# The second product of the plain chunks reads w_out in straight rows, and the columns are ordered on the way out, with a new table for the order of work

## Chip, core and metric

The kernel runs on one core of one Trainium2 chip. The metric is the time of one execution in microseconds, as the device sees it; the number for a kernel is the median of its runs. Beside the timed runs there is one execution under the profiler, whose trace the rows below are from.

## What is computed

Linear attention without softmax, an RMS norm per head, and a two-layer network with the gate h * cos(h). All inputs are float32: q, k, v of 8 x 8 x 576 x 64, w_in of 512 x 2048, w_out of 2048 x 512.

```python
kv = np.einsum('bhsd,bhse->bhde', k, v)
out = np.einsum('bhsd,bhde->bhse', q, kv)
rms = np.sqrt(np.mean(out * out, axis=-1, keepdims=True) + 1e-06)
attn = out / rms * g_norm
x = attn.transpose(0, 2, 1, 3).reshape(4608, 512)
h = x @ w_in
g = h * np.cos(h)
result = g @ w_out
```

## The kernel before

**Tiles.** The 4608 rows of x are nine chunks of 512 (`CH`), the inner width of 2048 is 16 blocks of 128 (`NJ`, index j), and a result is written in tiles of 128 rows x 512 columns (index t, four to a chunk). The float32 values are split into a high and a low part of type float32r (`hi`, `lo`), and each product is three matmuls: high by high, high by low, low by high. One such triple streams 512 columns three times.

**Stages.** Chunks 0 to 2 (`PLAIN = 3`) are done step by step: `stage1_part` makes h for one block j (the bank of its own, `bank` in the trace), `act_part` makes g = h * cos(h) and splits it into `ghi` and `glo`, and `stage2_part` adds g times the block of w_out into four PSUM banks `acc0` to `acc3`. Chunks 0 and 1 are cut into two segments each, since w_in and w_out are still being loaded: the first segment's result is stored in DRAM (`part`), and at the end of the second it is loaded again and added (`out_part` with `before`). Chunks 3 to 8 form three pairs. Their first product (`quad_part`) is done for two chunks at once by a scheme of seven products for eight blocks; its triples carry `bank<-wi,wo` in the trace, since its weight products are kept in the buffers named `wo` and its combinations of x in those named `wi`. The second product of chunks 3 to 6 (`gather_part`) is plain again, as in `stage2_part`; that of the last pair, chunks 7 and 8, goes through `turned_unit`, where w_out is the stationary operand and g the moving one.

**w_out's columns.** `w_part` converts each block of w_out from its 64-bit words and splits it; for w_out it writes `hi` and `lo` with the 16 groups of 32 columns in another order (a and b exchanged, 4 x 4), which the turned pair wants. The plain second product undoes this as it reads: `by_column(w[:, s, :])` is an access of 4 x 4 runs of 32 elements, and `acc` holds the columns in order. `out_part` then scales `acc` into a tile `slot` on ScalarE (or on DVE, added to `slot`, where there is a first part) and stores it; `t_slot` has five such tiles, which the norms of x and the sums of weights use as well. A tile goes back only when its store has landed.

**Order.** The order of instructions on each engine and of the DMA issues on SP is worked out by a planner in the kernel itself (`Order`), with a cost in us for each step (0.68 for a triple of matmuls of either product), a due time `due(i)`, and an offset for each step from the table `haste` (`put_off`). `grid` rounds the planned times, `sched.busy` holds the time from which an engine is free. What the planner decides is fixed: every instruction is issued in program order on its engine, through the one line 239 (`Pinned`), so in the trace all have the line L239, and groups are told apart by their tiles' names. `warm_part(16)` issues 64 matmuls on zeros into `acc2` at the front, where nothing else is ready. `sums_part` forms the sums of blocks of w_in for the quads.

Of the kernel before, what the change touches and what calls it, by code (L numbers as in the profile page):

```python
# [20 lines left out]
P = 128  # L21
# [29 lines left out]
def grid(t):  # L51
    return math.floor(t * 1e4 + 0.5) / 1e4
# [133 lines left out]
def tile_kernel(  # L186
# [42 lines left out]
    sched.busy["SP"] = sched.busy["DMA"] = 1.0  # L229
# [17 lines left out]
    def act_us(f=CH):  # L247
        return 0.1 + f / 1200
# [71 lines left out]
    def due(i):  # L320
# [7 lines left out]
        ('acc', 10): -397.3, ('acc', 11): 485.7, ('acc', 13): 49.6, ('acc', 14): 28.2, ('acc', 15): 71.1,  # L328
        ('acc', 16): -266.2, ('acc', 17): -172.1, ('acc', 18): 13.0, ('acc', 19): 2084.8, ('acc', 20): 23.3,
        ('acc', 21): 63.5, ('acc', 22): -52.9, ('acc', 23): 83.0, ('acc', 24): 343.6, ('acc', 25): 87.6,  # L330
        ('acc', 26): 343.7, ('acc', 27): 140.1, ('acc', 28): -2.0, ('acc', 29): 311.3, ('acc', 3): 389.0,
        ('acc', 30): -2.1, ('acc', 31): -258.8, ('acc', 32): -73.3, ('acc', 33): 146.9, ('acc', 34): -416.8,
        ('acc', 35): -518.1, ('acc', 36): -7.7, ('acc', 37): 434.6, ('acc', 38): 7.4, ('acc', 39): -253.4,
        ('acc', 4): -4.9, ('acc', 40): -84.3, ('acc', 41): 114.5, ('acc', 42): -117.7, ('acc', 43): 872.7,
        ('acc', 45): 464.5, ('acc', 46): 150.6, ('acc', 47): 168.2, ('acc', 5): -103.0, ('acc', 6): 292.7,
        ('acc', 7): -6.3, ('acc', 8): 205.3, ('acc', 9): 2.6, ('act', 0): 18.4, ('act', 1): -25.5,
        ('act', 10): 161.8, ('act', 11): 31.6, ('act', 12): -151.2, ('act', 13): -18.6, ('act', 14): -417.1,
        ('act', 15): -20.1, ('act', 16): -112.5, ('act', 17): -2.7, ('act', 18): -69.9, ('act', 19): 114.6,
        ('act', 2): -130.9, ('act', 20): -37.8, ('act', 21): 189.3, ('act', 22): -1.6, ('act', 23): 29.1,
        ('act', 24): -36.1, ('act', 25): -18.7, ('act', 26): 63.5, ('act', 27): -272.7, ('act', 28): -1.2,  # L340
        ('act', 29): 348.9, ('act', 3): -36.3, ('act', 30): -20.4, ('act', 31): 32.0, ('act', 32): -75.3,
        ('act', 33): 823.6, ('act', 34): -1.3, ('act', 35): -46.6, ('act', 36): -315.4, ('act', 37): 20.3,
        ('act', 38): -1.9, ('act', 39): 52.2, ('act', 4): 36.6, ('act', 41): 72.1, ('act', 42): 77.9,
        ('act', 43): 21.2, ('act', 44): -13.8, ('act', 45): -87.8, ('act', 46): 7.3, ('act', 47): -0.7,
        ('act', 5): -2.9, ('act', 6): -4.1, ('act', 7): 8.1, ('act', 8): -37.5, ('act', 9): 477.3,
        ('cross', 0, 0): 444.4, ('cross', 0, 1): 11.9, ('cross', 1, 0): 298.7, ('cross', 1, 1): 5.8,
        ('cross', 2, 0): -741.2, ('cross', 2, 1): -35.7, ('gate keep in', 0): -27.4, ('gate keep in', 1): 31.8,
        ('gate keep in', 10): -70.6, ('gate keep in', 11): 17.5, ('gate keep in', 12): -309.9,
        ('gate keep in', 13): -166.9, ('gate keep in', 14): 32.5, ('gate keep in', 15): -943.7,
        ('gate keep in', 2): -15.3, ('gate keep in', 4): 52.1, ('gate keep in', 5): 75.3,  # L350
        ('gate keep in', 6): 51.3, ('gate keep in', 7): -157.6, ('gate keep in', 8): -0.9,
        ('gate keep in', 9): -72.9, ('gate keep out', 0): 95.2, ('gate keep out', 1): 16.6,
        ('gate keep out', 10): 81.3, ('gate keep out', 11): 64.0, ('gate keep out', 12): 97.4,
        ('gate keep out', 13): -312.6, ('gate keep out', 14): -22.6, ('gate keep out', 15): -462.5,
        ('gate keep out', 2): -16.3, ('gate keep out', 3): -49.3, ('gate keep out', 4): 40.5,
        ('gate keep out', 5): -119.3, ('gate keep out', 6): 152.4, ('gate keep out', 7): 179.5,
        ('gate keep out', 8): 129.8, ('gate keep out', 9): 41.7, ('gate kv', 2): -38.9, ('gate kv', 3): 10.8,
        ('gate kv', 4): 20.0, ('gate kv', 5): -17.5, ('gate kv', 6): 56.5, ('gate kv', 7): -31.4,
        ('gate load', 2): -250.8, ('gate load', 3): -274.1, ('gate load', 4): -3.9, ('gate load', 5): 103.0,
        ('gate load', 6): -113.5, ('gate load', 7): -73.9, ('gate sums', 0): 22.8, ('gate sums', 2): 69.6,  # L360
        ('gate sums', 3): 3.0, ('gate sums', 4): -258.7, ('gate sums', 5): -3.5, ('gate sums', 6): 13.8,
# [1682 lines left out]
```

## Time and profile before

| | us |
|---|---|
| median of 3 timed runs | 878.9 (878.8 to 879.05) |
| the profiled execution | 875.54 |
| its span, first to last instruction | 873.8 |
| TensorE busy | 833.7 |
| DVE, ScalarE, POOL busy | 684.0, 521.0, 315.8 |

Times in rows are in us from the start of the span unless marked ns. A busy TensorE is counted as a union of pipelined matmuls, so the mean duration of one matmul is longer than the distance from one to the next; the distance is read from stretches of the chain. An engine executes in order, and an idle time is put down to what ended it.

### The profile page before, as it was taken

How to read it: one execution, taken by the hardware profiler on the slowest of the kernel's cores; microseconds unless marked ns; L12 is line 12 of the kernel's file. 1: busy time of each engine (PE TensorE's matmuls, PEld its weight loads, DVE VectorE, ACT ScalarE, POOL GpSimd, SP SyncE). 2: the span in 40 equal slices, each digit the busy share in tenths (PEclk: the TensorE clock that was granted, in tenths of full speed). 3: DMA queues.
4: the chain of work that ended last, by engine and by line, in shares of the span. 5: the costliest groups of instructions: out<-in, count | busy, mean ns of one | idle time of the engine just before them, and what ended most of it. 6: DMA issues, size and time to landing. Idle time of an engine off the chain costs nothing.

```text
span 873.8 us, 13064 instructions
## 1 busy us (share of the span) xinstructions
PE 833.7 (95%) x4392; PEld 676.0 (77%) x4392; DVE 684.0 (78%) x1034; ACT 521.0 (60%) x1019; POOL 315.8 (36%) x221
## 2 busy tenths in 40 slices
PE   7899999998998998999998999999998899999996
PEld 6678887887886886778886788878885788888875
DVE  2899997358576687766899898999679777788885
ACT  4789874346444565655677675786556555566550
POOL 2410044615436655000154482222157446553220
PEclk9999999999999999999999999999999999999999
DMA  9996255376773456779978856876566779796587
GB/s 307 304 399 243 83 163 177 122 199 175 225 192 111 124 169 218 216 253 357 271 217 223 257 171 181 230 230 194 179 195 206 237 205 298 262 342 195 171 286 192
DMA packets 175089, 191.70 MB, mean 219 GB/s; under 512 B 83376, under 2 KB 137136, under 8 KB 175024
## 3 DMA queue, kind: packets, MB, share of 16 engines
q1 hardware_dynamic: 173600, 190.04, 70.1%
q10 hardware_dynamic: 1424, 0.85, 0.3%
q8 instruction: 34, 0.56, 0.3%
q14 instruction: 31, 0.25, 0.1%
HBM read 143.66 MB, written 47.19 MB: 218 GB/s over the span
## 4 chain that ended last, share of the span: by engine, by line
PE 72%; DVE 12%; DMA 7%; ACT 4%; issue 3%; POOL 1%; SPq 0%; DVEq 0%; ACTq 0%; POOLq 0%
PE acc L239 37%; PE bank L239 35%; DVE sg L239 2%; DVE r L239 2%; DMA wo<-wod 2%; DMA wod<-wo 2%; DMA wo<-wq 2%; DVE wo L239 2%; DVE wi L239 1%; DVE glo L239 1%; DMA out_dram<-slot 1%; DVE m L239 1%; DVE qT L239 1%; DVE xhi L239 1%; DVE xlo L239 1%
## 5 line engine op out<-in xcount | busy, mean ns | idle before, releaser
L239 PE MATMUL acc<-wo,ghi 128*128 128x512 f32 x896 | 283.9, 398 | 4.2 <-DMA wo<-wod 3.0
L239 PE MATMUL bank<-wi,wo 128*128 128x512 f32 (+2 forms) x1092 | 245.6, 380 | 10.4 <-DMA wo<-wq 3.8
L239 PEld LDWEIGHTS bank<-wi,wo 128*128 128x128 f32 (+2 forms) x1092 | 190.1, 184 | 57.2 <-ACT wi L239 3.7
L239 PEld LDWEIGHTS acc<-wo,ghi 128*128 128x128 f32 x896 | 167.6, 189 | 44.1 <-issue 3.4
L239 POOL TENSOR_TENSOR rinv<-ms,mhalf 128x16 f32<-128x16 f32 (+1 forms) x36 | 97.9, 2721 | 280.1 <-DVE ms L239 278.4
L239 PE MATMUL acc<-wo,glo 128*128 128x512 f32 x448 | 178.3, 398 | 2.0 <-DVE glo L239 2.0
L239 PE MATMUL bank<-xhi,wi 128*128 128x512 f32 x320 | 102.4, 401 | 6.5 <-DVE r L239 3.9
L239 PEld LDWEIGHTS acc<-wo,glo 128*128 128x128 f32 x448 | 84.5, 189 | 23.1 <-DVE glo L239 2.8
L239 PEld LDWEIGHTS bank<-xhi,wi 128*128 128x128 f32 x320 | 60.8, 192 | 21.2 <-DVE r L239 4.3
L239 ACT ACTIVATE ki<-wi 128x512 int32<-128x512 f32 x72 | 45.1, 627 | 39.9 <-DVE wi L239 32.6
L239 DVE TENSOR_TENSOR wi<-bank,wi 128x512 f32<-128x512 f32 x72 | 49.0, 683 | 22.9 <-PE bank L239 16.6
L239 PE MATMUL bank<-xlo,wi 128*128 128x512 f32 x160 | 63.9, 400 | 0.0
L239 ACT ACTIVATE ki<-bank 128x512 int32<-128x512 f32 x72 | 42.6, 591 | 29.2 <-PE bank L239 20.4
L239 ACT COPY wi<-bank 128x512 f32<-128x512 f32 x72 | 42.0, 583 | 22.6 <-PE bank L239 19.7
L239 DVE SCALAR_TENSOR_TENSOR r<-bank,ki 128x512 f32<-128x512 f32 x49 | 33.5, 684 | 26.9 <-ACT ki L239 26.5
L239 DVE TENSOR_TENSOR glo<-r,ghi 128x512 fp32r<-128x512 f32 x55 | 44.5, 811 | 10.6 <-ACT ghi L239 10.3
L239 DVE TENSOR_TENSOR glo<-wo,ghi 128x512 fp32r<-128x512 f32 x46 | 38.3, 833 | 15.3 <-ACT ghi L239 15.1
L239 ACT CAST ghi<-wo 128x512 fp32r<-128x512 f32 x53 | 32.7, 618 | 27.8 <-PE acc L239 27.3
L239 ACT ACTIVATE r<-r 128x512 f32<-128x512 f32 x59 | 37.2, 630 | 16.8 <-DVE r L239 16.6
L239 ACT CAST ghi<-r 128x512 fp32r<-128x512 f32 x56 | 34.5, 618 | 20.2 <-PE acc L239 16.0
L239 ACT ACTIVATE wo<-wo 128x512 f32<-128x512 f32 x54 | 33.6, 630 | 21.1 <-DVE wo L239 21.0
L239 DVE TENSOR_TENSOR r<-r,bank 128x512 f32<-128x512 f32 x49 | 33.2, 678 | 8.4 <-ACT r L239 7.9
(217 smaller groups left out, 1447.5 us busy)
## 6 DMA issues: line engine op xcount, KB each, us to landing
wo<-wq SPq DMA_DIRECT2D x84, 512.0 KB, 4.3
wo<-wod SPq DMA_DIRECT2D x64, 512.0 KB, 4.5
wo<-in_moe_w_out_dram SPq DMA_DIRECT2D x16, 512.0 KB, 9.1
wi<-in_moe_w_in_dram SPq DMA_DIRECT2D x16, 512.0 KB, 9.2
wod<-wo SPq DMA_DIRECT2D x16, 512.0 KB, 3.9
wo<-wsum SPq DMA_DIRECT2D x32, 256.0 KB, 4.1
out_dram<-slot SPq DMA_DIRECT2D x28, 256.0 KB, 3.1
wq<-wi SPq DMA_DIRECT2D x24, 256.0 KB, 3.3
```

What stands on the lines that cost most here:

```text
L239: return lambda *a, **kw: tc.keep_in_program_order(f(*a, **kw))
```

## The change

`w_part` stays as it is, so w_out still lies in the exchanged order. The plain second product (in `stage2_part` and in `gather_part`) now reads it straight, `w[:, s, :]`, and `acc` holds exchanged columns. `out_part` puts them in order: on ScalarE one instruction reads `acc` in 4 x 4 runs of 32 and writes `slot` straight; on DVE, where a first part is added, four instructions take 128 columns each. A branch of `out_part` for chunk 8 is taken out. In `sums_part` a test is written in another way. `warm_part` gets 12 for 16. In the planner the rounding, the start values of SP and DMA and three costs of loads change, and the whole table `haste` is another (two lines of each stand here).

```diff
--- before.py
+++ after.py
@@ -49,7 +49,7 @@
 
 
 def grid(t):
-    return math.floor(t * 1e4 + 0.5) / 1e4
+    return math.floor(t * 1e4 + 0.43) / 1e4
 
 
 class Order:
@@ -226,7 +226,7 @@
     ps_s = ctx.enter_context(tc.tile_pool(name="ps_s", bufs=1, space=bass.MemoryType.PSUM))
 
     sched = Order()
-    sched.busy["SP"] = sched.busy["DMA"] = 1.0
+    sched.busy["SP"], sched.busy["DMA"] = 0.75, 1.9
 
     class Pinned:
 
@@ -325,156 +325,155 @@
 
 
     haste = {
-        ('acc', 10): -397.3, ('acc', 11): 485.7, ('acc', 13): 49.6, ('acc', 14): 28.2, ('acc', 15): 71.1,
-        ('acc', 16): -266.2, ('acc', 17): -172.1, ('acc', 18): 13.0, ('acc', 19): 2084.8, ('acc', 20): 23.3,
...
+        ('acc', 0): 14.0, ('acc', 1): -140.7, ('acc', 10): -107.5, ('acc', 11): -138.5, ('acc', 12): -36.8,
+        ('acc', 13): 292.5, ('acc', 14): -16.0, ('acc', 15): -12.0, ('acc', 16): 97.5, ('acc', 17): -604.7,
...
     }
 
     def put_off(*key):
@@ -603,7 +602,7 @@
                 if b:
                     yield copies(t[0:SP], heads.rearrange("h (p i) d -> p h i d", i=SQ), 1.1)
                 else:
-                    yield copies(t, heads.rearrange("h (p i) d -> (h p) i d", i=SF), 0.78)
+                    yield copies(t, heads.rearrange("h (p i) d -> (h p) i d", i=SF), 0.95)
         return pieces
 
     def first_loads():
@@ -626,7 +625,7 @@
                 copies(
                     qb[32 * e:32 * e + 32, o0 // 32:(o0 + n) // 32, :],
                     q[b, 2 * p + e // 2, s0:s0 + n, 32 * (e % 2):32 * (e % 2) + 32].rearrange(
-                        "(tb t) d -> t tb d", t=32), 0.14 + 0.18 * n / CH)
+                        "(tb t) d -> t tb d", t=32), 0.14 + 0.178 * n / CH)
                 for b, s0, o0, n in chunk_parts(c) for e in range(4)]
         return pieces
 
@@ -647,7 +646,7 @@
             for i, x in enumerate(pairs):
                 q_tiles[c, x] = qn[:, 2 * i:2 * i + 2]
             if c == 0:
-                yield copies(qn, q[0, heads, 0:CH, :].rearrange("h (r a) d -> r h a d", a=NTT), 0.78)
+                yield copies(qn, q[0, heads, 0:CH, :].rearrange("h (r a) d -> r h a d", a=NTT), 0.82)
             for b, r0, r1, m in front_rows(c):
                 if c:
                     r0 = (S - CH) // 2 if b and not m else r0
@@ -1202,10 +1201,6 @@
 
     accs = {}
 
-    def by_column(w):
-
-        return w.rearrange("p (b a r) -> p a b r", a=4, b=4)
-
     def stage2_part():
         for i, (c, j, first, final) in enumerate(steps):
             yield "wait", [w_done["wo", j], g_done[i]]
@@ -1220,7 +1215,7 @@
                 cols = slice(t * P, (t + 1) * P)
                 for n, (gt, s) in enumerate(((ghi, 0), (ghi, 1), (glo, 0))):
                     pe.matmul(
-                        out=accs[t], lhsT=gt[:, cols], rhs=by_column(w[:, s, :]),
+                        out=accs[t], lhsT=gt[:, cols], rhs=w[:, s, :],
                         start=(first and n == 0), stop=(final and n == 2),
                     )
                 if final:
@@ -1239,35 +1234,27 @@
 
     partial = {}
 
+    def by_column(acc):
+
+        return acc.rearrange("p (b a r) -> p a b r", a=4, b=4)
+
+    def in_order(o):
+        return o.rearrange("p (a b r) -> p a b r", a=4, b=4)
+
     def out_part(c, t, acc, complete, prio):
         before = partial.pop((c, t), None)
-        ends = c == NCH - 1
-        if ends and t == NTT - 1:
-
-            cut = DM // 2
-            halves = []
-            for _ in range(2):
-                slot = yield "take", t_slot, prio
-                halves.append(slot_tile(slot)[:, 0:cut])
-            yield "run", [("ACT", act_us(cut))], prio
-            act.activation(out=halves[0], in_=acc[:, 0:cut], func=AF.Copy, scale=OUT_SCALE)
-            act.dma_start(out=rows(c, t)[:, 0:cut], in_=halves[0])
-            yield "run", [("DVE", dve_us(cut))], prio
-            dve.tensor_scalar(out=halves[1], in0=acc[:, cut:], scalar1=OUT_SCALE, scalar2=None, op0=ALU.mult)
-            sp.dma_start(out=rows(c, t)[:, cut:], in_=halves[1])
-            return
         slot = yield "take", t_slot, prio
         o = slot_tile(slot)
         if before is not None:
             yield from dmas([copies(o, before, 0.85)], prio)
-            _, end = yield "run", [("DVE", dve_us(DM))], prio
-            dve.scalar_tensor_tensor(out=o, in0=acc, scalar=OUT_SCALE, in1=o, op0=ALU.mult, op1=ALU.add)
-        elif ends and t == NTT - 2:
-            _, end = yield "run", [("DVE", dve_us(DM))], prio
-            dve.tensor_scalar(out=o, in0=acc, scalar1=OUT_SCALE, scalar2=None, op0=ALU.mult)
+            for b in range(4):
+                _, end = yield "run", [("DVE", dve_us(P))], prio
+                whole = in_order(o)[:, :, b]
+                dve.scalar_tensor_tensor(
+                    out=whole, in0=by_column(acc)[:, :, b], scalar=OUT_SCALE, in1=whole, op0=ALU.mult, op1=ALU.add)
         else:
             _, end = yield "run", [("ACT", act_us(DM))], prio
-            act.activation(out=o, in_=acc, func=AF.Copy, scale=OUT_SCALE)
+            act.activation(out=in_order(o), in_=by_column(acc), func=AF.Copy, scale=OUT_SCALE)
         sched.give(t_acc[t], end)
         to = rows(c, t)
         if not complete:
@@ -1418,10 +1405,10 @@
             yield "run", [("POOL*", pool_us(WH))], prio
             pool.tensor_tensor(out=out, in0=a, in1=b, op=ALU.subtract)
         kept = []
-        for t, places in ((rest, (S2, S3)), (even, (S1, A22))):
-            slot = spare if t is rest else (yield "take", t_slot, prio)
+        for t, own, places in ((rest, spare, (S2, S3)), (even, None, (S1, A22))):
+            slot = own if own is not None else (yield "take", t_slot, prio)
             yield "run", [("ACT", act_us())], prio
-            if t is rest:
+            if own is not None:
                 hi = two(pair, [P, CH], F32R, 1)
             else:
                 hi = at.tile([P, CH], F32R, name=f"slot{slot}", bufs=1)
@@ -1896,7 +1883,7 @@
                 cols = slice(t * P, (t + 1) * P)
                 for n, (gt, s) in enumerate(((ghi, 0), (ghi, 1), (glo, 0))):
                     pe.matmul(
-                        out=accs[t], lhsT=gt[:, cols], rhs=by_column(w[:, s, :]),
+                        out=accs[t], lhsT=gt[:, cols], rhs=w[:, s, :],
                         start=(j == 0 and n == 0), stop=(j == NJ - 1 and n == 2),
                     )
                 if j == NJ - 1:
@@ -1943,7 +1930,7 @@
             t = due(begin[c]) - 24 + 1 * p if c else -10.0 + 0.5 * p
             sched.spawn(kv_front_part(c, p, t + put_off("kv", c, p)))
             sched.spawn(x_front_part(c, p, t + put_off("x", c, p)))
-    sched.spawn(warm_part(16))
+    sched.spawn(warm_part(12))
     for key in sorted(need, key=lambda x: (need[x], x)):
         t = due(need[key]) - 14.0 + put_off("load", *key)
         load(t, [w_in[key]], w_loads(key), wait=lent.get(key, ()))
```

## Rows read from the trace of the kernel before

**Rows 1.** The page's busy times, with shares of the span and instructions.

```profile
PE 833.7 (95%) x4392; PEld 676.0 (77%) x4392; DVE 684.0 (78%) x1034; ACT 521.0 (60%) x1019; POOL 315.8 (36%) x221
```

**Rows 2.** The page's chain that ended last, by engine and by line.

```profile
PE 72%; DVE 12%; DMA 7%; ACT 4%; issue 3%; POOL 1%; SPq 0%; DVEq 0%; ACTq 0%; POOLq 0%
PE acc L239 37%; PE bank L239 35%; DVE sg L239 2%; DVE r L239 2%; DMA wo<-wod 2%; DMA wod<-wo 2%; DMA wo<-wq 2%; DVE wo L239 2%; DVE wi L239 1%; DVE glo L239 1%; DMA out_dram<-slot 1%; DVE m L239 1%; DVE qT L239 1%; DVE xhi L239 1%; DVE xlo L239 1%
```

**Rows 3.** Windows: stretch, length, busy us of each engine, granted clock, DMA.

```profile
330.00:385.00 55.00, 48.59 (x206) 37.71 (x205) 38.66 (x55) 31.89 (x57) 10.46 (x10) 1.00 0.76 247
700.00:750.00 50.00, 50.00 (x218) 40.70 (x217) 38.23 (x53) 26.47 (x47) 29.49 (x25) 1.00 0.83 263
...
273.82:277.52 3.70, 3.69 (x10) 2.94 (x11) 3.62 (x7) 2.89 (x6) 3.31 (x4) 0.55 0.00 0
```

**Rows 4.** What TensorE waited for: us in total, times, longest.

```profile
PE bank L239 <- DVE r L239: 5.9, 3, 3.9
PE bank L239 <- DMA wo<-wq: 3.8, 3, 2.8
PE bank L239 <- issue: 3.4, 1, 3.4
PE acc L239 <- DMA wo<-wod: 3.0, 1, 3.0
...
PE acc L239 <- ACT slot L239: 1.0, 1, 1.0
```

**Rows 5.** Groups by shape: count, busy us, mean ns, idle before; plain second product.

```profile
L239 PE MATMUL acc<-wo,ghi 128*128 128x512 f32 x896 | 283.9, 398 | 4.2 <-DMA wo<-wod 3.0 <-ACT slot L239 1.0 <-ACT ghi L239 0.2
...
L239 PE MATMUL acc<-wo,glo 128*128 128x512 f32 x448 | 178.3, 398 | 2.0 <-DVE glo L239 2.0
```

**Rows 6.** The chain in order of time: start us, length us, what.

```profile
138.89 16.80 PE acc L239 x72
...
344.87 5.64 DMA wo<-wq
...
474.58 6.72 DMA wo<-wod
...
716.60 8.20 PE bank L239 x36
...
814.45 23.83 PE acc L239 x105
```

**Rows 7.** Groups by shape on ScalarE and DVE.

```profile
L239 ACT ACTIVATE slot<-acc 128x512 f32<-128x512 f32 x32 | 18.8, 601 | 7.2 <-PE acc L239 5.4 <-ACT wi L239 0.6 <-DMA out_dram<-slot 0.6
...
L239 ACT CAST wo<-sg 128x512 fp32r<-128x512 f32 x16 | 9.9, 617 | 4.3 <-DVE sg L239 4.2
L239 ACT CAST wi<-sg 128x512 fp32r<-128x512 f32 x16 | 9.9, 617 | 2.5 <-DVE sg L239 2.5
...
L239 DVE SCALAR_TENSOR_TENSOR ms<-part,swp 128x16 f32<-128x16 f32 x28 | 6.1, 216 | 4.8 <-ACT swp L239 4.7
...
L239 DVE SCALAR_TENSOR_TENSOR slot<-acc,slot 128x512 f32<-128x512 f32 x8 | 5.3, 674 | 0.0
...
L239 DVE TENSOR_TENSOR kv_w<-bank,kv_w 64x256 fp32r<-64x256 f32 x12 | 5.1, 422 | 5.4 <-ACT kv_w L239 5.1
```

**Rows 8.** TensorE in order of time: start, length, instruction, idle before.

```profile
29.98 0.84 PE L239 MATMUL acc<-zeros 128*128 128x128 bf16 x12
...
36.76 0.66 PE L239 MATMUL bank<-ident,r 128*128 128x128 f32 x4 [1.71 <-DVE r L239]
...
203.22 0.70 PE L239 MATMUL bank<-xhi,wi 128*128 128x512 f32 x2 [2.29 <-DVE slot L239]
...
273.82 1.22 PE L239 MATMUL bank<-xhi,wi 128*128 128x512 f32 x2 [3.88 <-DVE r L239]
```

**Rows 9.** SP's issues in order of time.

```profile
343.01 1.76 SPq L239 DMA_DIRECT2D out_dram<-slot  x2
344.87 0.38 SPq L239 DMA_DIRECT2D wo<-wq  x1
```

More of the change, by code (lines that the diff above doesn't have):

```diff
@@ L333, in tile_kernel @@
[L333 to L358, printed above, removed]
@@ L359, in tile_kernel @@
-        ('gate load', 2): -250.8, ('gate load', 3): -274.1, ('gate load', 4): -3.9, ('gate load', 5): 103.0,
-        ('gate load', 6): -113.5, ('gate load', 7): -73.9, ('gate sums', 0): 22.8, ('gate sums', 2): 69.6,
-        ('gate sums', 3): 3.0, ('gate sums', 4): -258.7, ('gate sums', 5): -3.5, ('gate sums', 6): 13.8,
-        ('gate sums', 7): 21.8, ('gate x', 2, 0): -386.5, ('gate x', 2, 1): -66.8, ('gate x', 2, 2): -4.1,
[17 rows of a table removed]
-        ('keep in', 7): -89.9, ('keep in', 8): -207.2, ('keep in', 9): 3.5, ('keep out', 0): 52.6,
@@ new lines, in tile_kernel @@
+        ('act', 7): 4.1, ('act', 8): -43.9, ('act', 9): -108.0, ('cross', 0, 0): 222.6, ('cross', 0, 1): 122.1,
+        ('cross', 1, 0): -9.9, ('cross', 1, 1): -421.9, ('cross', 2, 0): 33.3, ('cross', 2, 1): -5.3,
+        ('gate keep in', 0): 44.9, ('gate keep in', 1): -35.7, ('gate keep in', 10): -63.1,
+        ('gate keep in', 11): -234.5, ('gate keep in', 12): -376.8, ('gate keep in', 13): -51.0,
+        ('gate keep in', 14): 18.0, ('gate keep in', 15): -22.9, ('gate keep in', 2): -7.1,
@@ new lines, in tile_kernel @@
+        ('gate keep out', 5): 147.4, ('gate keep out', 6): -19.5, ('gate keep out', 7): 145.1,
+        ('gate keep out', 8): -551.2, ('gate keep out', 9): 35.4, ('gate kv', 3): -31.6, ('gate kv', 4): -66.4,
+        ('gate kv', 5): -8.0, ('gate kv', 6): 56.8, ('gate kv', 7): -122.6, ('gate load', 2): -23.5,
+        ('gate load', 3): 5.9, ('gate load', 4): -43.1, ('gate load', 5): 74.7, ('gate load', 6): -21.7,
+        ('gate load', 7): -9.9, ('gate sums', 0): 4.5, ('gate sums', 1): -3.2, ('gate sums', 2): 69.5,
@@ new lines, in tile_kernel @@
+        ('gate sums', 3): 28.8, ('gate sums', 4): -94.3, ('gate sums', 5): 36.0, ('gate sums', 6): -574.7,
+        ('gate sums', 7): -184.0, ('gate x', 2, 0): -316.2, ('gate x', 2, 1): -62.8, ('gate x', 2, 2): 4.3,
[16 rows of a table added]
+        ('keep out', 10): 260.9, ('keep out', 11): -1.1, ('keep out', 12): -1.1, ('keep out', 13): -37.0,
+        ('keep out', 14): -33.2, ('keep out', 15): -134.3, ('keep out', 2): 48.2, ('keep out', 3): 91.6,
+        ('keep out', 4): -73.2, ('keep out', 5): -537.0, ('keep out', 6): 21.3, ('keep out', 7): -276.1,
@@ new lines, in tile_kernel @@
+        ('keep out', 8): -61.1, ('keep out', 9): 80.0, ('kv', 0, 1): -174.7, ('kv', 0, 2): -183.2,
+        ('kv', 1, 0): -410.3, ('kv', 1, 1): -710.4, ('kv', 1, 2): 62.3, ('kv', 1, 3): 69.4, ('kvd', 3): -157.3,
+        ('kvd', 4): 245.1, ('kvd', 5): -119.0, ('kvd', 7): -36.2, ('kvs',): -4.8, ('kvt', 4): 201.8,
[12 rows of a table added]
+        ('load', 'wo', 9): 524.8, ('part', 2, 1, 0): 65.7, ('part', 2, 1, 1): -150.2, ('part', 2, 1, 3): 60.6,
+        ('part', 2, 1, 5): -0.6, ('part', 2, 1, 6): -0.8, ('part', 2, 1, 7): -29.8, ('part', 2, 2, 0): 243.1,
```

159 lines of the change are left out of this document (85 added, 74 removed), and 85 rows, old and new, of the table haste.

## Prediction

> **What bounds the kernel now.** I read the page first: TensorE is busy 833.7 us of a span of 873.8 us [rows 1], so 40.1 us are left in which it does nothing (before its first instruction and after its last included). Then the chain of work that ended last: 72% of it is TensorE, 37% matmuls into the banks `acc` and about as much matmuls into `bank`; DVE has 12% and DMA 7% [rows 2]. The reader is to see that no other engine holds the end over long stretches. The windows say where TensorE is full and where it isn't: from 700 to 750 us it is busy 50.00 us of 50, from 330 to 385 us only 48.59 of 55 [rows 3]. So a shorter matmul is worth its whole saving in the first kind of stretch, and is partly swallowed by the next wait in the second kind. Last, the list of who waited for whom on TensorE: 20 lines that sum to 32.9 us, the largest of them x chains on DVE (5.9) and loads of weight products (3.8) and of w_out (3.0) [rows 4].
>
> **The matmuls of the plain second product.** The groups by shape give their number: 896 with `ghi` and 448 with `glo`, 1344 in all, three for each of 448 output tiles and steps [rows 5]. These are the ones whose moving operand is w_out read by columns, in 16 runs of 32 elements. Their mean of 398 ns is a latency of pipelined instructions and no price. The price is read from the chain in order of time, where a stretch of nothing but such matmuls stands with its length: 72 in 16.80 us at 138.89 us, 233.3 ns each (a second stretch of 72, in the last plain chunk, has the same length) [rows 6]. The same view has the neighbours that stream 512 straight columns: 105 of the turned last pair, which write the same `acc` banks from the same kinds of tile (there w_out is the stationary operand), take 23.83 us, 227.0 ns each; 36 of the first product take 8.20 us, 227.8 ns [rows 6]. The three differ in which operand is stationary and in the pattern of the moving one. I put the 6.3 ns down to the pattern. The change makes it straight, so the term is 1344 x 6.3 = 8.5 us of TensorE time, with 1344 x 5.5 = 7.4 us by the nearer price of the first product.
>
> How much of it lies on the path? 37% of 873.8 us is 323 us of `acc` matmuls on the chain [rows 2]. The turned pair has 8 x 7 x 2 x 3 = 336 matmuls by the code, 76 us at 227 ns; if all of these are on the chain, 247 us are left for the plain ones, or 1059 of 1344 at 233.3 ns. These pay in full: 1059 x 6.3 = 6.7 us. The other 285 (1.8 us) stand ahead of waits that something else ends, and I count half. Term taken: -7.6 us; ends -5.8 (1059 x 5.5) and -8.5.
>
> The Trainium skill has a rule that speaks against this (SBUF — State Buffer, section "Door 1: The DMA port swizzle", its note on cachelines): accesses that stay in one 16-byte line of SBUF run at full bandwidth, and only crossing to a new line costs. A run of 32 float32 fills eight whole lines, so by it the reading by columns should be as fast as the straight row, and the term would be 0. The 233.3 against 227.0 ns speak against it, but no row shows w_out as a straight moving operand, so it is among the rivals.
>
> **Putting the columns in order on the way out.** 28 output tiles go through ScalarE, with four squarings of the front in the same group of 32, 601 ns each [rows 7]. Now ScalarE reads PSUM in runs of 32 and writes straight. The nearest rows are two copies of 128x512 on ScalarE, one with both sides in runs of 32 (`wo<-sg`) and one with both straight (`wi<-sg`): 617 and 617 ns [rows 7]. They read SBUF, not PSUM; still I take 0. From below nothing excludes a small gain, and the upper end is a doubling, +0.6 us each. Only where the next chunk waits for its bank is that on the path: TensorE waited 1.0 us in one place for such an output [rows 4]. With four tiles at one such place the end is +2.4 us.
>
> Eight output tiles of the split chunks 0 and 1 go through DVE, 674 ns each [rows 7]; each becomes four instructions of 128 columns. DVE takes 422 ns for 256 columns on 64 partitions and 216 for 16 columns [rows 7]; on the line from 674 (512) to 422 (256) that is 296 ns for 128, so 4 x 296 = 1184 ns, 0.51 us more a tile and 4.1 us of DVE in all (ends 4 x 216 = 0.86 and 4 x 422 = 1.69 us a tile). Queued behind them on DVE are the norm steps of chunk 2, whose slots wait for these stores: the one such stall, 2.29 us ahead of 203.22 us, is ended by a DVE write of a slot [rows 8]. I take +0.5 us (one tile's growth at that place), ends 0 and +4.1.
>
> **The rest of the edits.** The branch for the last chunk (halves on ScalarE and DVE) goes; chunk 8 is in the turned pair and never came here, so it removes no instruction. The rewritten test in the sums of w_in issues the same instructions. Sixteen of 64 warming matmuls go: 12 took 0.84 us at 29.98 us [rows 8], so about 1.1 us, and they are hidden by what follows, an idle of 1.71 us up to 36.76 us that DVE ends. Price 0; down to -1.1 us, and up to one more stretch at half clock. What that costs is seen at 273.82 us: after an idle of 3.88 us [rows 8] the granted clock over the next 3.70 us is 0.55 [rows 3], the lower level (1.2 GHz) for nearly all of it, and nine matmuls fill it (a tenth starts at its end) where 9 x 0.2278 = 2.05 us would do: 1.65 us lost.
>
> **The order of everything.** The new table of offsets, the rounding and the start values change every queue's order: SP's issues, POOL's adders, DVE, ScalarE and TensorE. No row prices an order that isn't there. What can be won is bounded by what stands idle: 32.9 us of waits less about 8 in the first 40 us (my count; 3.4 of issue is the largest [rows 4]), so 25 us, in a dozen places. They come in this manner: at 474.58 us the chain sits 6.72 us in a load of w_out, at 344.87 us 5.64 us in a load of weight products [rows 6]; and that load was issued only at 344.87 us because SP stood at two output stores from 343.01 us [rows 9]. Such a wait is a matter of two neighbours in a queue, and it can go or come with any new order. One thing speaks for a small gain: the planner counts 0.68 us for three matmuls of either product, which is 3 x 227, while the plain second product takes 3 x 233.3 = 0.70, so over 448 triples the chip falls 9 us behind the plan while transfers do not; after the change plan and chip have the same pace. I take -3 us, ends -12 (half of the 25) and +12 (waits of the body half as many again).
>
> **The sum**, against the profiled execution's own 875.54 us (span 873.8, 1.74 around it): 875.54 - 7.6 + 0 + 0.5 + 0 - 3 = 865.4 us. The median shown, 878.9, is 3.36 us above that execution; the forecast for the median is 865.4 + 3.4 = 868.8 us. A measurement of this kernel can tell about 0.2%, 1.8 us, from no change.
>
> **Rivals.** *The pattern is not what costs.* The 6.3 ns come from w_out being the moving operand at all, or from its place, and stay. Against it: the quads stream tiles of the same pool and take 227.8 ns; for it: no row isolates the pattern. Then 875.54 + 0.5 - 3 + 3.4 = 876.4 us. This is also the case in which the change does not do what it says.
>
> *The new order also clears waits.* If half of the 25 us go, 12 instead of 3: 868.8 - 9 = 859.8 us. For it: the waits are few and long, three of them 3.9, 3.0 and 2.8 us [rows 4]. Against it: a shorter matmul uses up weights sooner, and a load on the path takes 5 to 7 us [rows 6].
>
> *Slower: loads and stores cross on SP in the new order.* Place: the change from the plain chunks to the quads, 330 to 385 us, where TensorE already loses 6.4 us [rows 3] because a load stands behind a store that waits for ScalarE, which waits for a slot. A faster TensorE arrives there 2 to 3 us sooner and finds the same transfers. Each crossing costs what the ones of now cost, 2.8 to 3.9 us of wait, and with an idle of 3.88 us another 1.65 of half clock. The saving of 7.1 (7.6 less 0.5) is used up by two such places and the result is slower by over 1.8 us from three on: 3 x 3.3 = 9.9, without the order's 3: 878.9 - 7.1 + 9.9 = 881.7 us, and up to 886 with four and their half clock.
>
> *A little worse order.* One or two crossings more: 875 to 880 us.
>
> **Chances.** Forecast (pitch falls, order between +2 and -8 against none; 863.8 to 873.8) 0.60; order clears more, 856 to 864: 0.12; one or two crossings 0.11, of which 0.06 are still below 877.1; pattern without effect 0.09 (0.05 of it below 877.1); slower 0.08. So faster 0.83, same 0.09, slower 0.08. The range is 860 to 878: below it lies half of the second case (0.06), above it the slower one and about half of the two that end near 878.
>
> **What would show it.** The chain's stretches of `acc` matmuls before the turned pair: 72 in 16.3 us show the pattern's price, 16.8 refute it. `slot<-acc` on ScalarE near 601 ns; on DVE 32 pieces near 296 ns. TensorE's waits sum to about 30 us; over 45 would be the slower rival, and its releasers (DMA of `wo`, slots) say which place. A stretch at 1.2 GHz after an x chain, as at 273.82 us, would show that the order kept such a wait. I would be wrong if `acc` matmuls keep 233 ns, if the output tiles of chunk 0 or 1 hold up their banks, or if the waits grow at the place named.

## The result and the profile after

The changed kernel takes 847.63 us in the median (843.72 to 848.52, four runs) against 878.85 (876.41 to 879.05): a ratio of 0.964 [0.961, 0.968]. The forecast was 868.8 us in a range of 860 to 878. The sign was right, the size was not: 31 us were won where 10 were foretold. The experiments below were run against the kernel before in sessions of their own, whose medians for it lie between 875.2 and 877.0 us; so a difference of two medians from two sessions is good to 2 us or so, and the ratios stand beside them.

The page of the changed kernel, its first part (busy time and number of instructions of each engine), answers to [rows 1]:

```profile
span 846.7 us, 13061 instructions
PE 820.8 (97%) x4376; PEld 673.1 (79%) x4376; DVE 691.2 (82%) x1062; ACT 521.4 (62%) x1018; POOL 316.9 (37%) x218
```

The span is 27.1 us shorter. TensorE's busy time gives 12.9 us of that, and the time in which it does nothing falls from 40.1 to 25.9 us, which gives 14.2. Of this second half the forecast had hardly anything. The waits of TensorE, answering to [rows 4] (who waited for whom: us in total, times, longest), sum to 18.7 us in 13 lines, against 32.9 in 20; the largest:

```profile
PE bank L239 <- DVE r L239: 3.2, 2, 1.7
PE bank L239 <- DVE wo L239: 2.6, 2, 1.5
PE acc L239 <- DVE r L239: 2.6, 3, 2.0
PE bank L239 <- ACT wi L239: 2.1, 2, 1.4
PE bank L239 <- DMA wo<-wq: 1.8, 2, 1.2
PE acc L239 <- DMA wo<-wod: 0.4, 1, 0.4
```

The three long ones of before (3.9 for an x chain, 2.8 for weight products, 3.0 for w_out) are gone; no wait is longer than 2.0 us. The chain of waits (start, length, what), answering to [rows 6], has the price of a plain matmul: 51 in 11.56 us and 90 in 20.42 us are 226.7 and 226.9 ns each, where it was 233.3. A first-product stretch of 36 has 226.7 where [rows 6] gave 227.8:

```profile
679.63 8.16 PE bank L239 x36
690.51 11.56 PE acc L239 x51
713.65 20.42 PE acc L239 x90
```

The groups by shape (count, then busy us and mean ns of one), answering to the outputs of [rows 7], show ScalarE at 595 ns where it was 601, and DVE at 278 ns for a piece of 128 columns, four of them 1112 ns where one of 512 took 674:

```profile
L239 ACT ACTIVATE slot<-acc 128x512 f32<-128x512 f32 x32 | 18.5, 595 | 3.0 <-PE acc L239 2.7
L239 DVE SCALAR_TENSOR_TENSOR slot<-acc,slot 128x128 f32<-128x128 f32 x32 | 7.4, 278 | 0.4 <-DMA slot<-part 0.3
```

Last, the granted clock. Before, TensorE falls to the lower level (1.2 GHz) at 14.3, 38.2, 273.7 and 481.9 us, for 3.4 us each time, and at the end; after, at 331.2 us only, and at the end. Three windows of before have such a stretch in them (the one at 273.7 us is in [rows 3]):

```profile
12.00:18.00 6.00, 4.28 (x76) 4.09 (x76) 0.83 (x2) 1.23 (x6) 0.54 (x1) 0.72 1.10 324
36.00:42.00 6.00, 4.93 (x16) 3.80 (x17) 5.99 (x11) 2.63 (x5) 1.64 (x1) 0.72 1.07 386
481.00:486.00 5.00, 4.56 (x15) 3.78 (x16) 3.33 (x6) 1.93 (x4) 0.26 (x1) 0.66 1.03 315
```

The windows of the changed kernel (busy time of each engine, then the granted clock), of which the first two hold the places where before had it at the front, and the third the one that is left:

```profile
12.00:18.00 6.00, 3.90 (x100) 3.38 (x100) 2.86 (x7) 2.84 (x9) 1.66 (x1) 1.00 1.09 349
36.00:42.00 6.00, 5.86 (x46) 4.20 (x44) 6.00 (x12) 5.55 (x13) 1.62 (x1) 1.00 1.07 374
331.20:334.60 3.40, 3.40 (x9) 2.64 (x9) 1.91 (x3) 1.69 (x3) 0.12 (x1) 0.51 0.55 167
```

In the third window 9 matmuls fill 3.4 us at a clock of 0.51; in the 3.4 us behind it there are 16 at 0.99. So a stretch costs about 1.7 us, and three fewer are 5 us of the 12.9 by which TensorE is less busy. The rest, 7.8 us, is near the pattern's price, 1344 x 6.6 ns = 8.9 us.

Where the time was won shows when both traces are counted by progress. The table gives, in us, when so much of the matmul work was done (columns streamed / 512, warming left out; 3466 in all). It is from one traced execution of each kernel. It has two experiments of the next section: e1 is before with straight rows alone, e2 is the changed kernel with the columns read as before.

| work done | before | e1 | e2 | after |
|---|---|---|---|---|
| 69 | 42.5 | 44.1 | 39.2 | 38.0 |
| 341 | 107.5 | 108.3 | 109.2 | 105.7 |
| 749 | 206.4 | 208.3 | 206.3 | 201.3 |
| 1020 | 274.6 | 275.7 | 270.8 | 265.7 |
| 1428 | 377.0 | 378.7 | 367.6 | 363.7 |
| 1971 | 512.9 | 514.9 | 500.6 | 495.0 |
| 2651 | 676.2 | 678.9 | 658.8 | 652.7 |
| 3466 | 866.7 | 867.1 | 847.6 | 839.7 |

TensorE's waits in the stretches between (sums of the lines that the view gives for each window):

| window, us | before | e1 | e2 | after |
|---|---|---|---|---|
| 0 to 42 | 8.1 | 8.8 | 7.1 | 5.1 |
| 42 to 240 | 3.7 | 4.1 | 4.6 | 4.4 |
| 240 to 300 | 3.9 | 3.9 | 0.3 | 0.6 |
| 300 to 400 | 6.3 | 6.8 | 2.9 | 3.5 |
| 400 to 640 | 4.5 | 6.8 | 3.3 | 4.0 |
| 640 to 760 | 6.1 | 5.3 | 0.4 | 0.4 |

The new order (e2 against before) is level at 206 us and then gains about 4, 6, 3 and 5 us in the four stretches in which the waits of before go, with what half clock follows them. The lead of 3 us that its front has at 42 us is lost again by 107.

### The profile page after: what moved, and what is told of

Read it like the earlier page. It is cut to its first block, busy times and chain, and to the rows that moved or that the text cites. A ratio compares the mean times of both kernels' runs of the same rounds, so it can differ in the third digit from the quotient of the medians.

```text
span 846.7 us, 13061 instructions
## 1 busy us (share of the span) xinstructions
PE 820.8 (97%) x4376; PEld 673.1 (79%) x4376; DVE 691.2 (82%) x1062; ACT 521.4 (62%) x1018; POOL 316.9 (37%) x218
## 4 chain that ended last, share of the span: by engine, by line
PE 66%; DVE 18%; DMA 6%; ACT 4%; issue 3%; POOL 1%; SPq 1%; DVEq 0%; ACTq 0%; POOLq 0%
PE bank L239 35%; PE acc L239 31%; DVE sg L239 4%; DVE wi L239 3%; DVE wo L239 2%; DVE r L239 2%; DMA wo<-wq 2%; DVE glo L239 2%; POOL rinv L239 1%; DVE slot L239 1%; DMA x<-slot 1%; DMA k_over<-in_k_dram 1%; DMA qb<-in_q_dram 1%; DVE ms L239 1%; ACT slot L239 1%
## 5 line engine op out<-in xcount | busy, mean ns | idle before, releaser
L239 PE MATMUL acc<-wo,ghi 128*128 128x512 f32 x896 | 278.5, 392 | 0.5 <-DVE wo L239 0.5
L239 POOL TENSOR_TENSOR rinv<-ms,mhalf 128x16 f32<-128x16 f32 (+1 forms) x36 | 101.6, 2826 | 205.9 <-DVE ms L239 204.5
L239 PE MATMUL acc<-wo,glo 128*128 128x512 f32 x448 | 175.2, 391 | 0.4 <-DVE glo L239 0.4
L239 PE MATMUL bank<-xhi,wi 128*128 128x512 f32 x320 | 100.0, 392 | 0.7 <-DVE wi L239 0.6
L239 PEld LDWEIGHTS acc<-wo,glo 128*128 128x128 f32 x448 | 84.2, 188 | 19.3 <-DVE glo L239 1.7
L239 ACT CAST ghi<-wo 128x512 fp32r<-128x512 f32 x49 | 30.1, 616 | 21.7 <-PE acc L239 21.3
L239 ACT CAST ghi<-r 128x512 fp32r<-128x512 f32 x56 | 34.5, 618 | 14.2 <-PE acc L239 10.2
L239 DVE TENSOR_TENSOR glo<-r,ghi 128x512 fp32r<-128x512 f32 x53 | 38.8, 736 | 4.8 <-ACT ghi L239 4.3
L239 PE MATMUL acc<-wi,wo 128*128 128x512 f32 x162 | 38.0, 390 | 0.3 <-DVE m L239 0.3
```

Source lines behind the costliest of these rows:

```text
L239: return lambda *a, **kw: tc.keep_in_program_order(f(*a, **kw))
```

## Experiments

The first question was whether the two halves, the straight rows and the new order, have each their own worth, or whether the order can be cleared only because plan and chip now run at one pace (the argument of the prediction's order step; theories A and B in the first two expectations). Each half was made alone. An expectation's "theory" is a reading with what it would make of the time.

**e1: straight rows in the order of before.** Every queue keeps the order of before; the output is put in order as in the change.

```diff
-                        out=accs[t], lhsT=gt[:, cols], rhs=by_column(w[:, s, :]),
+                        out=accs[t], lhsT=gt[:, cols], rhs=w[:, s, :],
...
-            act.activation(out=o, in_=acc, func=AF.Copy, scale=OUT_SCALE)
+            act.activation(out=in_order(o), in_=by_column(acc), func=AF.Copy, scale=OUT_SCALE)
...
```

> The kernel before with the straight rows and the ordering on the way out alone; every queue keeps the order of before (the four DVE pieces stand where the one instruction stood). Theory A, pattern and order add up: 1344 matmuls fall from 233.3 to about 227 ns, 6.7 to 8.9 us of it on the path, so 870 to 872 us; the waits of TensorE stay near 33 us and the rest of the 31 us is the new order's. Theory B, one pace: the waits of the old order were there because the chip fell behind its plan, and go with it: 862 us or less, waits under 25 us. Rival, the pattern costs nothing: 879 us, matmuls still at 233 ns.

Measured: 872.73 us (nine runs) against 876.97, ratio 0.994 [0.991, 0.997]. The chain of e1 has the pattern's price whole, 72 matmuls in 16.32 us, 226.7 ns each, the stretch that took 16.80 in [rows 6]:

```profile
140.07 16.32 PE acc L239 x72
744.87 16.32 PE acc L239 x72
```

Its list of waits has the three long ones with larger sums than in [rows 4] (5.9, 3.8 and 3.0), and adds up to 35.8 us where before has 32.9 (the traced execution of e1 is the slowest of its nine, 875.77 us):

```profile
PE bank L239 <- DVE r L239: 6.3, 3, 3.9
PE bank L239 <- DMA wo<-wq: 4.9, 4, 2.6
PE acc L239 <- DMA wo<-wod: 3.9, 1, 3.9
PE bank L239 <- issue: 3.6, 1, 3.6
```

So the pattern is 4 to 5 us in this order, about half of its 8.9. That the shorter matmul arrives sooner at the same transfers, and they take some of the gain back, fits these sums, but they are of one execution each and don't show it. The one pace of plan and chip clears none of the long waits.

**e2: the new order, columns read as before.** The changed kernel with `by_column` back at the matmuls and straight outputs.

```diff
-                        out=accs[t], lhsT=gt[:, cols], rhs=w[:, s, :],
+                        out=accs[t], lhsT=gt[:, cols], rhs=by_column(w[:, s, :]),
...
```

> The changed kernel with w_out read by columns as before, output tiles written straight, DVE in one instruction instead of four; every queue keeps the new order. Theory A: 1344 x 6.6 ns = 8.8 us slower than the changed kernel, 855 to 857 us, waits of TensorE near its 18 us. Theory B: the chip falls behind the plan again and the waits come back, 865 us or more. Rival, the pattern costs nothing: 848 us.

Measured: 854.16 us, ratio 0.974 [0.970, 0.978]. Its chain has 233.3 ns again, in the same stretch of 51 that takes 11.56 us in the changed kernel:

```profile
697.01 11.90 PE acc L239 x51
720.51 21.00 PE acc L239 x90
```

Its waits sum to 19.2 us, with TensorE busy for 828.3. The new order is worth 22.8 us without the straight rows, the straight rows 6.5 us on top of it (854.16 - 847.63; 8.7 by the two ratios). The halves alone make 27.0 of the 31.2 us, so they add, but for some 4 us that lie near the noise between sessions; theory B fell. Span times granted clock tells how much of it is half clock (the span multiplied by the run's mean granted clock, and the rest of the span as lost; idle time is weighed too, so this is a reckoning), as medians of the runs:

| | span x clock, us | lost to the clock, us |
|---|---|---|
| before | 864.9 | 10.1 |
| e1, straight rows | 859.0 | 11.3 |
| e2, new order | 848.5 | 3.8 |
| after | 840.3 | 4.2 |

By this reckoning 16 us of the order's gain are time at full clock, waits above all, and 6 are clock. The two traces say much the same: e2's span is 19.3 us shorter than that of before, 13.9 of it idle time of TensorE (its listed waits fall by 13.7) and 5.4 busy time. The straight rows are 8 us at full clock in the new order, 6 in the old.

**e3 and e4: the table of offsets.** e3 is before with the new table alone. e4 is the changed kernel with an empty table.

The diff of e3 against before, cut to its first lines:

```diff
     haste = {
-        ('acc', 10): -397.3, ('acc', 11): 485.7, ('acc', 13): 49.6, ('acc', 14): 28.2, ('acc', 15): 71.1,
+        ('acc', 0): 14.0, ('acc', 1): -140.7, ('acc', 10): -107.5, ('acc', 11): -138.5, ('acc', 12): -36.8,
...
```

The diff of e4 against the changed kernel, likewise:

```diff
-    haste = {
-        ('acc', 0): 14.0, ('acc', 1): -140.7, ('acc', 10): -107.5, ('acc', 11): -138.5, ('acc', 12): -36.8,
...
+    haste = {}
```

> The kernel before with the new table of offsets alone: old load costs, start values, warming matmuls and one planned DVE step of 512 columns, so the planner makes a third order out of the same offsets. If the offsets themselves are good whatever the planner's costs: about 856 us, as the new order with reading by columns. If they are good only together with the costs for which they were made: the waits of TensorE are back to 30 us or more, 870 to 890 us.

> The changed kernel with an empty table: the planner's own due times alone make the order; straight rows as in the changed kernel. If the order is worth little over what due times give: within 15 us of the changed kernel, 850 to 863 us. If the table carries the order: waits of TensorE of 60 us or more, above 890 us.

e3 took 870.68 us (ratio 0.992 [0.989, 0.995]; waits 30.7 us), e4 883.79 (1.008 [1.003, 1.012]; waits 46.0, and 22.5 us lost to the clock). So the table is worth 36 us in the changed planner, and the same table in the old planner is 16.5 us worse than in the new (e2, also with columns). e3 came out as its second reading had it; e4 came out between its two, with less harm than the 890 us foretold for a table that carries the order. The rounding and the start values of SP and DMA leave the order of every queue as it is, and e11 below shows the warming to be without effect, so what is left of the planner's edits are the three costs of loads and the output's four DVE steps.

**e7 and e8: these two, one at a time.** In e7 the three costs of loads are those of before; in e8 the output on DVE is planned as one step of 512 columns (the instructions are the same four).

The first of e7's three lines, then e8's edit:

```diff
-                    yield copies(t, heads.rearrange("h (p i) d -> (h p) i d", i=SF), 0.95)
+                    yield copies(t, heads.rearrange("h (p i) d -> (h p) i d", i=SF), 0.78)
```

```diff
+            _, end = yield "run", [("DVE", dve_us(DM))], prio
             for b in range(4):
-                _, end = yield "run", [("DVE", dve_us(P))], prio
```

> The changed kernel with the planner's three old costs of loads (0.78, 0.18, 0.78 for 0.95, 0.178, 0.82); table and all else new. The orders differ in 218 of some 3950 places on TensorE. Theory E, offsets and costs are a pair: waits come back in part, 855 to 870 us. Rival, the offsets carry the gain by themselves: 846 to 852 us.

> The changed kernel with the planner counting one DVE step of 512 columns for an output with a first part, as before, while the four instructions stay; the orders differ in 276 places on TensorE. Theory E: 855 to 870 us. Rival: 846 to 852 us.

e7 took 854.4 us (0.977 [0.973, 0.981]), e8 856.45 (0.979 [0.976, 0.981]). By progress e7 is 7.4 us behind the changed kernel at 341 of the work (113.1 against 105.7 us) and 6.0 behind at 1700; e8 is level until 1020 (267.3 against 265.7), 8.1 behind at 1292 and 7.0 at 1700. The list of waits of e8, from 300 to 345 us, has the place:

```profile
PE acc L239 <- DVE glo L239: 3.1, 1, 3.1
PE bank L239 <- DVE r L239: 0.9, 1, 0.9
```

The offsets belong to the costs they were made with: 7 and 9 us for a few tenths of a microsecond in the plan. Together that is about the 16.5 us between e2 and e3, though no run has both and nothing else. And what is lost at one place is mostly kept to the end, since TensorE is full from there on.

**e5 and e6: the transfers on SP.** The slower rival had loads and stores crossing on SP. e5 is e1 with the loads of q in one issue for four or eight (other values of q are loaded; 180 issues fewer on SP); e6 is e1 with the stores of outputs issued by ScalarE.

First e5's edit, then e6's:

```diff
...
+            one = copies(qb.rearrange("p a b -> p (a b)"), whole, pieces[-1][0])
+            return [one if i == len(pieces) - 1 else (us, late, lambda: None) for i, (us, late, _) in enumerate(pieces)]
```

```diff
...
+        if own:
+            act.dma_start(out=to, in_=o)
...
```

> The old order with straight rows (as e1), but each load of q from chunk 2 on is one issue of straight rows of 2 KB instead of four or eight of 128-byte runs; 180 issues leave SP, and nothing else moves in any queue. It reads the q rows in another layout, so its x and its output are of other values; the work is the same. Theory C, the old order's long waits come from loads of w_out that stand in SP's queue behind small loads (as at 474 us): the waits of TensorE fall by 4 us or more and the time by 6 or more against e1, to 866 us or less. Rival D, the waits come from chains of ScalarE and DVE, whatever SP does: within 2 us of e1.

> The old order with straight rows (as e1), but the 28 stores of output tiles that ScalarE made are issued by ScalarE right after it instead of by SP; the rest of the order is the same. The prediction's place for crossings, a load behind a store on SP at 343 us: the wait for the weight products there (2 to 3 us) goes, the time falls by 2 to 4 us against e1. Rival: ScalarE pays 28 x 0.4 us for the issues and the slots are held just as long: no change within 2 us, or slower.

e5: 870.22 us, ratio 0.993 [0.991, 0.996], which is e1's ratio. The wait of 3.9 us for w_out fell to 0.9, and the longest for weight products grew from 2.6 to 3.9:

```profile
PE bank L239 <- DVE r L239: 6.3, 3, 3.9
PE bank L239 <- DMA wo<-wq: 5.1, 3, 3.9
```

So 180 issues fewer on SP are worth nothing that can be measured here. e6: 881.51 us, ratio 1.006 [1.003, 1.009], 9 to 11 us worse than e1 by the medians or the ratios. Its list of waits has 41.3 us, some of them where the output's slot is late:

```profile
PE acc L239 <- ACT slot L239: 2.8, 2, 2.0
PE bank L239 <- DVE slot L239: 3.0, 1, 3.0
```

The waits for weight products are 5.9 us where e1 has 4.9, so taking the stores off SP does not free the loads. Whether more output tiles would was not tried.

**e9 and e10: the x chain.** The longest wait of before ends with a write of `r` by DVE; POOL's power for the norm (2.95 us each in before, 3.02 in the changed kernel, for 16 columns) is a step of that chain. e9 (on e1) and e10 (on the changed kernel) raise only one column of 16 to the power, so the other norms are left out; it takes 0.60 us in e9 and 0.65 in e10, and the plan is the same.

```diff
...
-        rinv = small.tile([P, TB], F32, name="rinv")
-        pool.tensor_tensor(out=rinv, in0=ms, in1=mhalf, op=ALU.pow)
+        rinv = rinvs[(NP * c + p) % 4]
+        pool.tensor_tensor(out=rinv[:, 0:1], in0=ms[:, 0:1], in1=mhalf[:, 0:1], op=ALU.pow)
```

> The old order with straight rows (as e1); POOL raises one column of 16 to the power -1/2 in each norm of chunk 2 and on (the other 15 factors stay 1, so the output has other values), about 1 us for 2.95. Every queue keeps its order. Theory F, the old order's long wait at 269 us is DVE standing at a norm step until POOL's power is done, with the steps of g that free the banks behind it: that wait (3.9 us) and the one at 200 us shrink to under half, waits of TensorE from 35 to 30 or less, and 4 to 8 us less than e1, with the stretch of half clock behind them. Rival, they hang on slots and on ScalarE: within 2 us of e1.

> The changed kernel with the same short power on POOL; every queue keeps the new order. If the new order has the power's latency hidden: within 2 us of the changed kernel, 845 to 849 us. If it stands on it too: 4 us or more faster, 843 or less.

e9: 877.44 us, ratio 1.001 [0.999, 1.004]; e10: 854.39, 0.976 [0.973, 0.979]. The list of waits of e9 keeps the 3.9 us, at 273.5 us where e1 has them at 275.2:

```profile
PE bank L239 <- DVE r L239: 5.0, 4, 3.9
PE bank L239 <- DVE slot L239: 2.0, 1, 2.0
```

The power's length is not what sets that wait. But both kernels were slower than their parents, by 5 and 7 us, which no expectation had, and the reason stands in the chain of e10: 51 straight plain matmuls in 11.87 us, 232.7 ns, the price of the columns.

```profile
616.68 11.87 PE acc L239 x51
692.69 11.86 PE acc L239 x51
```

Two things could have brought it: the values (most norms are left out), or the place of the tiles, since the tiles for `rinv` went from one pool to another and moved those of g (by the sizes in the code 128 bytes on, with w_out's tiles 256 bytes on).

**e14, e12, e13, e15: values or place.** e14 is the changed kernel with the norms' power set to 0 (so no norm is applied) and no tile moved. e12 and e13 add an unused tile of 128 and of 256 bytes to a partition ahead of the pool that holds `ghi` and `glo`, so that they lie that far on against w_out's tiles. e15 is e12 with the columns read as in e2.

```diff
+    pad = small.tile([P, 32], F32, name="pad", bufs=1)
+    pool.memset(pad, 0.0)
```

> The changed kernel with the norm's power 0 in place of -1/2, so every row keeps its length and the output has other values; every instruction, queue and address is the same. If the values cost (rival I, as e10's were of this kind too): 232 ns in the plain triples and 854 us. Theory G and rival H: 227 ns, 846 to 849 us.

> The changed kernel with an unused tile of 128 bytes per partition ahead of the tiles of g (ghi, glo, r, ki), which so start 128 bytes later while the tiles of w_out and x stay; every queue keeps its order but for one more memset on POOL. Theory G, the 6 ns are a matter of where the two operands of a matmul lie to each other: the straight plain triples are back at 232 to 233 ns, those of the turned pair whose g lies in the same tiles too, quads and the first product stay at 227; 854 to 856 us. Rival H, the pattern alone: 227 ns, 846 to 849 us.

> As e12 with 256 bytes. Theory G gives a change of the plain triples here or in e12, and does not say at which distance it stops. Rival H: 227 ns and 846 to 849 us in both.

> The new order with w_out read by columns (as e2) and the tiles of g 128 bytes later. If reading by columns costs by its jumps: still 233 ns, 853 to 856 us. If it costs by where the operands lie to each other (theory G): another mean than 233.4, and if it falls to 227, 846 to 849 us, and the straight rows weren't needed for the gain.

| kernel | median, us | ratio | a straight row or columns, ns of a plain matmul |
|---|---|---|---|
| after | 847.63 | 0.964 [0.961, 0.968] | straight, 226.7 |
| e14, no norms | 845.83 | 0.966 [0.963, 0.969] | straight, 226.7 |
| e12, 128 bytes on | 853.93 | 0.975 [0.971, 0.979] | straight, 232.7 |
| e13, 256 bytes on | 849.67 | 0.970 [0.964, 0.976] | straight, 226.7 |
| e2, columns | 854.16 | 0.974 [0.970, 0.978] | columns, 233.3 |
| e15, columns, 128 bytes on | 855.04 | 0.976 [0.973, 0.980] | columns, 233.3 and 236.7 |

The chain of e12, where the first product keeps 36 in 8.18 us while the plain stretches take what the columns took:

```profile
682.23 8.18 PE bank L239 x36
693.17 11.87 PE acc L239 x51
716.66 20.92 PE acc L239 x90
```

The chain of e13:

```profile
688.90 11.56 PE acc L239 x51
712.04 20.40 PE acc L239 x90
```

The chain of e15:

```profile
693.95 11.90 PE acc L239 x51
717.47 21.30 PE acc L239 x90
```

The values cost nothing. A straight row is cheap only where the g tiles lie well; 128 bytes on, nearly the whole gain of the straight rows is gone (853.93 us against the 854.16 of e2). The columns are dear at both places tried. Other distances were not tried.

The turned pair shows more of it. There g is the moving operand and w_out the stationary one, and 24 of its matmuls in a row that move `ghi` and `glo` take 226.7 ns each in the changed kernel and 232.9 in e12:

```profile
735.43 5.44 PE acc L239 x24
738.95 5.59 PE acc L239 x24
```

Those of the same pair that move `wi` tiles, which e12 leaves in place, keep 227. So the price goes with the place of the g tiles, whichever operand they are.

**e11: the warming.** The changed kernel with 16 groups for 12.

```diff
-    sched.spawn(warm_part(12))
+    sched.spawn(warm_part(16))
```

> The changed kernel with 16 groups of warming matmuls instead of 12; all queues but TensorE's have the same order, TensorE's differs by the 16 matmuls. Forecast's price for them 0: within 1.5 us of the changed kernel. Rival: they delay the front (1 us) or hold the clock up there (1.65 us less); more than 1.5 us either way.

847.56 us, ratio 0.968 [0.965, 0.970]: no difference to the changed kernel that the noise lets be seen, so the four groups are given the price 0.

## Why the prediction was right and wrong

**The pattern: right in its price, right by luck in its cause.** Forecast 6.3 ns a matmul and -7.6 us, measured 6.6 ns and -6.5 us in the new order (e2 against after; -8.7 by the ratios), -4.2 in the old (e1). That part of it is swallowed by waits was in the step, as 285 of 1344 at half; in the old order about half of the whole was lost. The rival that the 6.3 ns stay fell with e1; place, which it named beside the pattern, has a part all the same. For the step set straight against columns and nothing else, from rows whose tiles lay well by chance; e12 shows the same straight rows at 232.7 ns, so the pattern was worth its price only because the change left the g tiles where they were. That the turned pair took 227 in [rows 6] hung on the same place, as its stretches of 24 show; for the quads it was not tried.

The Trainium skill's rule on cachelines (SBUF — State Buffer, section "Door 1: The DMA port swizzle", its note) would have had runs of 128 bytes as fast as a straight row. e1 and e2 show 6.6 ns of 233.3 between the two at this place of the g tiles, so here the measurement differs from the rule, and it decides.

**The outputs: right.** ScalarE's 595 ns against 601 is as good as the 0 that was taken. DVE's pieces measured 278 ns where 296 were estimated from the line through two rows; the tile grew by 0.44 us against 0.51. At the stall that the step named, e1 has the four pieces in the order of before and waits 2.21 us at 203.5 us, where before waited 2.29 [rows 8]; so the +0.5 was not seen there. In the new order e2 (one DVE instruction a tile) and the changed kernel (four) both have about 4.5 us of waits between 42 and 240 us, as the table shows.

**The warming: right** within the noise, by e11.

**The order: the step that failed.** The term was -3 us with an end of -12; it is -22.8 by e2, and this alone is the miss: 865.4 with -22.8 for -3 gives 845.6 for the profiled execution, where 848.5 was measured. The mechanism it named, waits of TensorE that go with another order, is what was seen; the size, a part that was left out, and the reason were wrong.

First, the size. The step said that 25 us of waits could be won, took half as the end, and then -3 as the value, for which it had the one pace of plan and chip and no row. The waits that went are 13.7 us (e2) and 14.2 (after), the front included, which the 25 leave out; so the end of -12 was nearly what came, and the -3 was the guess that failed. The four windows from 240 to 760 us, where the waits named in the step lie, hold 6.9 us in e2 and 8.5 after, for 20.8 before.

Second, the clock. The paragraph before it worked out 1.65 us of half clock behind one idle of 3.88 us [rows 3, 8], priced it for the warming and for the slower rival, and left it out of the order's gain. The trace of before has four such stretches, each behind an idle of TensorE, that of e2 has two, and that of the changed kernel one. Six of the 22.8 us are of this kind by span times clock, and the medians of the runs, 11.3 us lost in e1 and 3.8 in e2, show that it is the order which removes them.

Third, the reason. The one thing said for a gain, that plan and chip fall apart by 9 us and the change brings them to one pace, is refuted by both halves: e1 has the pace and 35.8 us of waits, e2 has not and 19.2.

**The rivals.** "The new order also clears waits" (859.8, a chance of 0.12) is what happened: its 12 us are close to the waits that went, and the whole is twice its size, with the clock. The slower one, crossings on SP between 330 and 385 us, did not come: the waits of 300 to 400 us fell from 6.3 to 3.5. Its mechanism was not seen to rule either: e5 removes 180 issues from SP and wins nothing, e6 takes the stores off and loses 9 us or more. Which neighbour makes each wait of before is not settled: e5 shortens the wait for w_out by 3.0 us and lengthens one for weight products by 1.3 without a gain in time, e9 leaves the x chain's wait as it was. What is shown is that the order as a whole makes them.

**The range.** It ended at 860 because the order's end was cut to 12 us without clock. With all of the four places (20.8 us) and their half clock (3 x 1.7) as the end it would have reached 846 (868.8 + 3 - 20.8 - 5.1), and the measured 847.6 would lie just inside. That is said in hindsight: no order here cleared all four places.

## What to carry to other kernels

When a change brings a whole new order with it, price the order as its own part, with the waits that two neighbours in a queue can make and the half-clock stretches behind them as the possible gain; here 14 of 33 us of waits went, and some 6 us of clock with them. When a static order was made with certain costs, keep both together: the same offsets in the planner with the old costs lost 16 us of 23. Before a matmul's price is put down to an access pattern, shift one operand's tile by 128 bytes and look again.

## What was not expected of the hardware

**Where the operands lie.** The same matmul, the same straight row of 512 float32r columns: 226.7 ns with the g tiles at one place, 232.7 with them 128 bytes on, 226.7 with 256 bytes on (after, e12, e13). The first product, whose own two operands are elsewhere, keeps 227 in e12. The turned pair's matmuls that move g do the same (226.7 and 232.9). So the price goes by the place of the g tiles. Whether it is their place against the other operand or their place by itself is not shown, since in none of these runs does the other operand's tile move alone (in e10 g moves 128 bytes and w_out 256, with the same 232.7); why is open.

**Which idle brings the lower clock.** In the timeline of the changed kernel (start, length, what, idle before it) TensorE falls at 331.2 us to the lower level after idles of 0.68 and 1.03 us, a microsecond apart, where in before it did so after idles of 3.88 and 3.0 us:

```profile
328.46 0.73 PE L239 MATMUL bank<-wi,wo 128*128 128x512 f32 x2 [0.68 <-ACT wi L239]
330.22 1.23 PE L239 MATMUL bank<-wi,wo 128*128 128x512 f32 x4 [1.03 <-DVE wi L239]
```

A long idle is neither needed nor enough. The same trace passes idles of 1.99 and 1.73 us, at 15.6 and 43.7 us, without a fall. Before passes 2.29 us at 203.2 and 2.75 at 350.6 at full clock, where e1, in the same order, falls at 204.0 and 350.8 us, at idles of 2.21 and 2.63 us. e14, with the queues of the changed kernel, has an idle of 1.02 us at 328.8 us and no fall there, but one at 55.9. So the places differ from execution to execution, and what a new order brings in clock is better taken from several runs, as in the table of span times clock, than from one trace.
